# Splitting 4 KB of each row of one K load into sixteen small loads in a two-layer decode kernel

## The chip, the core and the metric

The kernel runs on one core of a Trainium2 chip. The core has a matrix engine (TensorE; PE in the profile, PEld for its weight loads), a vector engine (VectorE; DVE), a scalar engine (ScalarE; ACT), GpSimd (POOL) and SyncE (SP), which here does nothing but issue loads. Sixteen DMA engines move data between the chip's main memory (HBM) and the on-chip memory of 128 rows (partitions). The metric is the time of one execution in microseconds on the device; lower is better.

## What is computed

Two decode layers for 4 sequences, each an attention block with a cached K and V (8 groups of 4 query heads, 4096 cached positions, head size 128) and a gated feed-forward block, all in float32:

```python
def _A_ref(x, k_cache, v_cache, wq, wo):
    q = ...  # (x @ wq), split into 32 heads
    k = jnp.repeat(k_cache, rep, axis=1)
    v = jnp.repeat(v_cache, rep, axis=1)
    scores = jnp.einsum("bhqd,bhkd->bhqk", q, k) * (Dh ** -0.5)
    p = _softmax(scores, axis=-1)
    o = jnp.einsum("bhqk,bhkd->bhqd", p, v)
    return (lambda x, *d: x.transpose(*d))(o, 0, 2, 1, 3).reshape(B, Sq, Hq * Dh) @ wo
...
x = A_x
x = x + _A_ref(_layernorm(x, axis=-1), A_k_cache, A_v_cache, A_wq, A_wo)
x = x + _B_ref(_layernorm(x, axis=-1), B_w1, B_w3, B_w2)
x = x + _A_ref(_layernorm(x, axis=-1), A_k_cache, A_v_cache, A_wq, A_wo)
x = x + _B_ref(_layernorm(x, axis=-1), B_w1, B_w3, B_w2)
return x
```

Both layers use the same weights and the same cache. The cache is far larger than the on-chip memory: K and V are 8 MB each for one group, 128 MB in all, and are read once in each layer, apart from what is kept on chip between the layers.

## The kernel before

**The arena and the plan of loads.** All large data go through one tile, `arena`, of 212 KB in each of the 128 rows (lines 30, 31 and 46; `KB = 256` is a count of float32 elements, so 1 KB). The first 64 KB hold wq, the rest is handed out and taken back by `take` and `give`. A list, `plan` (lines 69 to 117), names every load in the order in which it is to be issued: source, the blocks (keys) that it brings, and a fixed place or none. `pump` (line 122) goes along this list: while there is room for the next load it issues it on SP (line 129) and notes where each key lies. When the last reader of a load has been issued, `done` or `vacate` gives the room back and calls `pump` again. The instructions are written out in this order by hand, and each engine runs its own in that order: SP issues one load after the other, and one that has to wait holds all that follow.

**The start of the plan.** Ahead of it ACT issues x without its first eight rows (line 156). Then SP issues the first 8 KB per row of wq, the first eight rows of x (line 132), the two halves of K of group 0 (32 KB per row each), the rest of wq (56 KB), K of group 1 (64 KB, 8 MB in all: the second K load, key `("k", 0, 1, 0)` and seven more), V of group 0, K of group 2 and so on. These up to K of group 1 find room at once; V of group 0 needs the room of K of group 0.

**Semaphores.** A load signals its landing on a semaphore. The framework gives the loads eight such semaphores in turn, in the order of the program, those of SP and the one of ACT together; the kernel does not say which load gets which, and the waits that come from it are the framework's.

**The work around it.** `project_q` (line 297) makes the first group's queries from the first part of wq; `scores` (line 330, matmuls in line 339) takes K of group 0, and then `q_product` (line 279, matmuls in line 283) makes the queries of the other seven groups when the rest of wq is there. Softmax (line 345) and the transposes of `turn_p` follow, then `scores` of group 1. From there on each group's scores are followed by `weigh` (line 374, matmuls in line 380) of the group before, with its V. A group's eight blocks of K are 8 KB per row each; in a block, the four sequences take 2 KB per row each.

Of the kernel before, what the change touches and what calls it, by code (L numbers as in the profile page):

```python
# [29 lines left out]
KB = 256  # L30
# [2 lines left out]
AGAIN = (0,)  # L33
SPLIT = 3
SCRATCH = 64


@with_exitstack
def tile_decode_layers(ctx: ExitStack, tc: tile.TileContext, x, kt, v, wq, wo, w1, w3, w2, out):
    nc = tc.nc  # L40
# [5 lines left out]
    arena = const.tile([P, ARENA * KB], F32, name="arena")  # L46
# [5 lines left out]
    def take(n, at=None):  # L52
        if at is not None and at < WO:
            return at
        for i, (lo, size) in enumerate(free):
            a = lo if at is None else at
            if lo <= a and a + n <= lo + size:
                free[i:i + 1] = [(p, s) for p, s in ((lo, a - lo), (a + n, lo + size - a - n)) if s]
                return a
        return None  # L60
# [61 lines left out]
    def pump():  # L122
        while state["next"] < len(plan):
            src, per, keys, at = plan[state["next"]]
            n = src.shape[-1] // KB
            a = take(n, at)
            if a is None:
                return
            nc.sync.dma_start(arena[:, a * KB:(a + n) * KB], src)
            i = state["next"]  # L130
            if i == 0:
                nc.sync.dma_start(xt[:8], x[:8])
            left[i] = (len(keys), a, n)
            for j, key in enumerate(keys):
                where[key] = (a + j * per, per, i)
            state["next"] += 1
# [5 lines left out]
    def done(*key):  # L142
        i = where[key][2]
        k, a, n = left[i]
        left[i] = (k - 1, a, n)
        if k == 1:
            give(a, n)
            pump()

    def vacate(*key):  # L150
        a, n, _ = where[key]
        give(a, n)
        pump()

    xt = const.tile([P, KC, B], F32, name="xt")
    nc.scalar.dma_start(xt[8:], x[8:])
    pump()

    ident = const.tile([P, P], F32, name="ident")
# [407 lines left out]
```

## Time and profile before

| | us |
|---|---|
| median of 3 runs | 711.67 |
| lowest and highest | 710.67, 712.11 |
| the profiled execution | 712.24 |
| its span, first to last instruction | 710.5 |
| PE busy in it | 417.6 (59%) |
| DVE busy | 76.3 (11%) |
| ACT busy | 38.6 (5%) |
| read from HBM | 299.90 MB, 422 GB/s over the span |

The profile is that of one execution. Its views are: a page with busy times, 40 equal slices of the span (busy shares in tenths, DMA share and GB/s), DMA queues and the chain of work that ended last, followed back from the last instruction; a view of instructions in order of time (start, duration, engine and line, operation, output and input, count); issues of loads with their size and the time from issue to landing, for any stretch; busy times by stretches; and who waited for whom. A "q" behind an engine's name is its sequencer, which issues loads and waits. All times are in microseconds from the first instruction.

### The profile page before, as it was taken

Reading aid. Unit: us, or ns where it says so; the run is one execution under the profiler, and the core shown is the slowest. Engines: PE = TensorE matmul, PEld = TensorE weight load, DVE = VectorE, ACT = ScalarE, POOL = GpSimd, SP = SyncE. Lnnn points to the kernel's source line nnn. Section 1 sums busy time; section 2 is a strip of 40 time slices with the busy share of each in tenths; the row PEclk is TensorE's granted clock in tenths of the full one; section 3 lists DMA queues with packets and bytes.
Section 4 is the critical chain, followed back from the end, with each engine's and each line's share of the span. In section 5 each row is a group of like instructions: output and inputs, shape, how many; then the busy total and the mean of one; then the engine's idle time right before and its main releaser. Section 6 shows DMA issues by size and latency. Waiting matters only on the chain.

```text
span 710.5 us, 7260 instructions
## 1 busy us (share of the span) xinstructions
PE 417.6 (59%) x3282; PEld 150.3 (21%) x3282; DVE 76.3 (11%) x270; ACT 38.6 (5%) x87; POOL 2.9 (0%) x10
## 2 busy tenths in 40 slices
PE   4545454546565554548578884265655636356878
PEld 2111121212121121212243221021211202121246
DVE  2010111111111010111011110111010011111111
ACT  0000000000000000001010000000000000001001
POOL 0000000000000000000000000000000000000000
PEclk9876776777676687779899997587787879788679
DMA  9999999999999999999999999999999999999995
GB/s 384 458 399 469 414 443 433 428 440 428 433 443 422 435 440 421 440 415 423 411 401 394 413 434 448 432 429 433 443 429 432 440 424 433 446 403 428 427 424 225
DMA packets 13862, 300.43 MB, mean 423 GB/s; under 512 B 1672, under 2 KB 1800, under 8 KB 6024
## 3 DMA queue, kind: packets, MB, share of 16 engines
q1 hardware_dynamic: 13696, 299.96, 98.7%
q8 instruction: 26, 0.43, 0.2%
q14 instruction: 5, 0.03, 0.0%
q10 hardware_dynamic: 135, 0.01, 0.0%
HBM read 299.90 MB, written 0.07 MB: 422 GB/s over the span
## 4 chain that ended last, share of the span: by engine, by line
DMA 69%; PE 26%; another core or an unknown queue 2%; DVE 1%; ACT 1%; issue 1%; SPq 0%; ACTq 0%; DVEq 0%
DMA arena<-in_v 29%; DMA arena<-in_kt 27%; PE o_ps L380 11%; PE s_ps L339 8%; DMA arena<-in_wq 6%; DMA arena<-in_wo 4%; DMA arena<-in_w 3%; PE q_ps L283 1%; PE d_ps L227 1%; PE s_ps L423 1%; ACT t L387 1%; PE m_ps L265 1%; PE x_ps L401 1%; PE o_ps L423 0%
## 5 line engine op out<-in xcount | busy, mean ns | idle before, releaser
L380 PE MATMUL o_ps<-arena,pT 128*32 128x512 f32 x1024 | 150.3, 737 | 144.6 <-DMA arena<-in_v 132.0
L339 PE MATMUL s_ps<-arena,qpad 128*32 128x512 f32 x1024 | 153.5, 755 | 89.9 <-DMA arena<-in_kt 89.9
L380 PEld LDWEIGHTS o_ps<-arena,pT 128*32 128x32 f32 x1024 | 38.2, 132 | 254.5 <-issue 224.8
L339 PEld LDWEIGHTS s_ps<-arena,qpad 128*32 128x32 f32 x1024 | 40.0, 134 | 186.6 <-issue 172.8
L389 DVE SCALAR_TENSOR_TENSOR t<-o_ps,parts,t 128x512 f32<-128x512 f32 x16 | 12.0, 751 | 266.7 <-PE o_ps L380 266.7
L346 DVE TENSOR_REDUCE top<-s_ps 128x1 f32<-128x512 f32 x16 | 11.1, 691 | 205.1 <-PE s_ps L339 205.1
L348 ACT ACTIVATE p<-s_ps,top 128x512 f32<-128x512 f32 x16 | 11.0, 687 | 315.1 <-DVE top L346 315.1
L392 PE MATMUL m_ps<-sel,t 128*128 128x16 f32 x128 | 17.0, 265 | 14.3 <-DVE t L389 14.2
L401 PE MATMUL x_ps<-arena,oT 128*4 128x256 f32 x256 | 18.8, 431 | 8.7 <-DMA arena<-in_wo 6.8
L387 ACT ACTIVATE t<-o_ps,parts 128x512 f32<-128x512 f32 x16 | 11.0, 687 | 212.6 <-PE o_ps L380 212.6
L283 PE MATMUL q_ps<-arena,xpad 128*32 128x512 f32 x112 | 14.8, 650 | 11.9 <-DMA arena<-in_wq 11.9
L392 PEld LDWEIGHTS m_ps<-sel,t 128*128 128x128 f32 x128 | 15.5, 191 | 29.1 <-DVE t L389 29.1
L227 PE MATMUL d_ps<-ident,rows 128*32 128x128 f32 x102 | 16.8, 288 | 0.0
L368 PE MATMUL t_ps<-ident,p 128*128 128x128 f32 x64 | 10.8, 293 | 4.5 <-ACT p L348 4.5
L227 PEld LDWEIGHTS d_ps<-ident,rows 128*32 128x32 f32 x102 | 11.7, 116 | 4.6 <-issue 0.5
L369 DVE COPY pT<-t_ps 128x512 f32<-128x512 f32 x16 | 11.0, 690 | 12.5 <-PE t_ps L368 12.5
L423 PE MATMUL s_ps<-arena,xpad 128*32 128x192 f32 (+1 forms) x128 | 9.7, 422 | 1.8 <-DMA arena<-in_w 1.5
L401 PEld LDWEIGHTS x_ps<-arena,oT 128*4 128x4 f32 x256 | 6.1, 92 | 17.3 <-DMA arena<-in_wo 7.3
L368 PEld LDWEIGHTS t_ps<-ident,p 128*128 128x128 f32 x64 | 7.6, 155 | 9.0 <-issue 5.1
L423 PE MATMUL o_ps<-arena,xpad 128*32 128x192 f32 (+1 forms) x128 | 8.1, 360 | 2.1 <-DMA arena<-in_w 2.0
L283 PEld LDWEIGHTS q_ps<-arena,xpad 128*32 128x32 f32 x112 | 3.5, 119 | 20.8 <-DMA arena<-in_wq 12.9
L401 PE MATMUL x_ps<-arena,hT 128*4 128x256 f32 x56 | 4.3, 379 | 2.8 <-DMA arena<-in_w 2.4
(96 smaller groups left out, 129.5 us busy)
## 6 DMA issues: line engine op xcount, KB each, us to landing
arena<-in_kt SPq DMA_DIRECT2D x4, 4096.0 KB, 21.0
arena<-in_v SPq DMA_DIRECT2D x4, 4096.0 KB, 40.2
arena<-in_kt SPq DMA_DIRECT2D x9, 1024.0 KB, 11.0
arena<-in_w SPq DMA_DIRECT2D x15, 512.0 KB, 7.4
arena<-in_wq SPq DMA_DIRECT2D x1, 7168.0 KB, 39.5
arena<-in_v SPq DMA_DIRECT2D x3, 2048.0 KB, 39.9
arena<-in_wo SPq DMA_DIRECT2D x1, 4096.0 KB, 25.2
arena<-in_kt SPq DMA_DIRECT2D x2, 2048.0 KB, 22.4
```

The lines of the kernel that those rows point to most:

```text
L227: nc.tensor.matmul(d_ps[0:32, :], rows, ident, start=True, stop=True)
L283: nc.tensor.matmul(ps[32 * k:32 * k + 32, :], xpad[:, k, lo:lo + 32], w[:, k, :], start=first, stop=last)
L339: nc.tensor.matmul(s_ps[32 * b:32 * b + 32, :], qpad[:, b, lo:lo + 32], k[:, j, :], start=(blk == 0), stop=(blk == NB - 1))
L346: nc.vector.tensor_reduce(top[:, 0:1], s_ps, axis=AX.X, op=ALU.max, negate=True)
L348: nc.scalar.activation(p, s_ps, AF.Exp, bias=top[:, 0:1], accum_out=l)
L368: nc.tensor.transpose(t_ps[:, i, :], p[:, i * P:(i + 1) * P], ident)
L380: nc.tensor.matmul(o_ps[32 * b:32 * b + 32, :], pT[:, i, 32 * b:32 * b + 32], w[:, b, :], start=(i == 0), stop=(i == NI - 1))
L387: nc.scalar.activation(t, o_ps, AF.Copy, scale=st["parts"][:, 0:1])
L389: nc.vector.scalar_tensor_tensor(t, o_ps, st["parts"][:, 1:2], t, op0=ALU.mult, op1=ALU.add)
L392: nc.tensor.matmul(flat(m), t[:, j * P:(j + 1) * P], sel[:, j].rearrange("p h b -> p (h b)"), start=(j == 0), stop=(j == 3))
L401: nc.tensor.matmul(x_ps[r:r + B, e * 256:e * 256 + 256], left(2 * i + n), w(n)[:, e * 256:e * 256 + 256], start=first, stop=last)
L423: nc.tensor.matmul(ps[32 * j:32 * j + 32, lo:lo + n], x32[:, k, :], w[:, j * n:(j + 1) * n], start=(k == 0), stop=(k == KC - 1))
```

## The change

One load of the plan, the second K load of layer 0, is issued in seventeen parts. The first 4 KB of each of its 128 rows go in sixteen loads, over rows 0 to 14, 15 to 28, and so on with 15, 14, 13 down to 1 row, and a last one of 8 rows (15 + 14 + ... + 1 + 8 = 128). The other 60 KB of each row follow in one load of 128 rows. Place in the arena, bytes and all other loads are as before. PE's waits follow from what its matmuls read.

```diff
+SHARED = ("k", 0, 1, 0)
...
             a = take(n, at)
             if a is None:
                 return
-            nc.sync.dma_start(arena[:, a * KB:(a + n) * KB], src)
             i = state["next"]
+            if keys[0] == SHARED:
+
+                r = 0
+                for m in (*range(15, 0, -1), 8):
+                    nc.sync.dma_start(arena[r:r + m, a * KB:(a + 4) * KB], src[r:r + m, 0:4 * KB])
+                    r += m
+                nc.sync.dma_start(arena[:, (a + 4) * KB:(a + n) * KB], src[:, 4 * KB:])
+            else:
+                nc.sync.dma_start(arena[:, a * KB:(a + n) * KB], src)
             if i == 0:
                 nc.sync.dma_start(xt[:8], x[:8])
```

## The prediction

> **What bounds the kernel now.** The page first: the rows by slices and the summary of the chain that ended last.
>
> ```profile
> span 710.5 us, 7260 instructions
> ...
> DMA  9999999999999999999999999999999999999995
> GB/s 384 458 399 469 414 443 433 428 440 428 433 443 422 435 440 421 440 415 423 411 401 394 413 434 448 432 429 433 443 429 432 440 424 433 446 403 428 427 424 225
> ...
> DMA 69%; PE 26%; another core or an unknown queue 2%; DVE 1%; ACT 1%; issue 1%; SPq 0%; ACTq 0%; DVEq 0%
> ```
>
> The DMA engines are busy in every slice but the last, and the chain is a row of loads. Next the table by stretches of time, for one long stretch of layer 0 and for the last microseconds of the loads.
>
> ```profile
> 82.00:324.00 242.00, 132.42 (x916) 41.74 (x916) 22.81 (x72) 12.19 (x27) 0.00 (x0) 0.74 1.00 432
> ...
> 700.00:704.20 4.20, 4.20 (x67) 3.56 (x55) 0.50 (x2) 0.29 (x2) 0.00 (x0) 1.00 0.54 213
> ```
>
> The last two columns are the busy share of the 16 DMA engines and GB/s. In 242 us the share is 1.00 at 432 GB/s, 27.0 GB/s for one engine: the queue never runs dry. The second row shows that the 16 engines do not finish together: 46% of 4.2 us, 1.9 us for the mean engine, is idle at the end because some are done before others. So two things can move the time: a gap in the stream of loads, which costs what it is long, and a better share-out among the engines, which can give 1.9 us at most.
>
> Then the place of the change: SP's issues, in the view in order of time, and the chain at that place.
>
> ```profile
> 0.74 0.37 SPq L129 DMA_DIRECT2D arena<-in_wq  x1
> 1.16 0.36 SPq L132 DMA_DIRECT2D xt<-in_x  x1
> 1.57 0.82 SPq L129 DMA_DIRECT2D arena<-in_kt  x2
> 2.43 0.45 SPq L129 DMA_DIRECT2D arena<-in_wq  x1
> 2.92 0.49 SPq L129 DMA_DIRECT2D arena<-in_kt  x1
> 30.06 0.33 SPq L129 DMA_DIRECT2D arena<-in_v  x1
> ```
> ```profile
> 2.43 39.46 DMA arena<-in_wq
> 41.90 0.04 issue
> 41.94 7.69 PE q_ps L283 x56
> ...
> 54.26 8.39 another core or an unknown queue
> 62.66 0.14 issue
> 62.79 10.01 PE s_ps L339 x64
> ```
>
> The second K load (8 MB, issued at 2.92) stands in the queue behind the rest of wq, which lands at 2.43 + 39.46 = 41.89. Its own bytes flow from then on and land at about 62.6, where PE starts its scores. Between 2.92 and 30.06 SP has nothing to issue.
>
> **What a load waits for before it is issued.** Eight completion semaphores are taken in turn by all loads, so the load eight places on takes the same one. Whether it waits for that, the middle of the kernel shows, where many loads are in flight. First the issue view of the stretch from 303 to 330.4 us (count, KB, us to landing; 1+1+2+1+1+2 = 8 loads), then single issues.
>
> ```profile
> arena<-in_wo SPq DMA_DIRECT2D x1, 4096.0 KB, 25.2
> arena<-in_v SPq DMA_DIRECT2D x1, 2048.0 KB, 27.0
> arena<-in_v SPq DMA_DIRECT2D x2, 1024.0 KB, 29.4
> arena<-in_wo SPq DMA_DIRECT2D x1, 2048.0 KB, 27.4
> arena<-in_wo SPq DMA_DIRECT2D x1, 1024.0 KB
> arena<-in_wo SPq DMA_DIRECT2D x2, 512.0 KB, 29.9
> ```
> ```profile
> 303.40 0.33 SPq L129 DMA_DIRECT2D arena<-in_v  x1
> ...
> 319.90 0.33 SPq L129 DMA_DIRECT2D arena<-in_wo  x1
> ...
> 330.42 0.33 SPq L129 DMA_DIRECT2D arena<-in_w  x1
> ...
> 345.10 0.33 SPq L129 DMA_DIRECT2D arena<-in_w  x1
> ```
>
> The load issued at 303.40 (2048 KB) lands at 303.40 + 27.0 = 330.40, and the ninth load, counted from it, goes out at 330.42. The one of 319.90 lands at 319.90 + 25.2 = 345.1, and the load eight places on goes out at 345.10. So a load is held until the load eight places ahead has landed, and SP, which issues in order, holds everything behind it.
>
> **The change, part by part.** Count all loads from the start: 0 is x on ACT, 1 the first wq, 2 the eight rows of x, 3 and 4 the halves of K 0, 5 the rest of wq. Before, the second K load is number 6. Now 6 to 21 are the sixteen pieces and 22 is the remaining 60 KB of each row. Piece j is load 5+j and waits for load j-3. Loads 1 to 5 and the second K load in the issue view, stretch by stretch:
>
> ```profile
> arena<-in_wq SPq DMA_DIRECT2D x1, 1024.0 KB, 4.8
> ...
> xt<-in_x ACTq DMA_DIRECT2D x1, 7.5 KB, 4.7
> ...
> arena<-in_kt SPq DMA_DIRECT2D x2, 4096.0 KB, 18.3
> ...
> arena<-in_wq SPq DMA_DIRECT2D x1, 7168.0 KB, 39.5
> ...
> arena<-in_kt SPq DMA_DIRECT2D x1, 59.7
> ```
>
> Pieces 1 and 2 go out at once, 3 to 5 at about 5.5, 6 and 7 after the halves of K 0 (median 18.3 us to landing). Piece 8 waits for load 5, the rest of wq: it can go out at 41.94 at the earliest. At that moment only pieces 1 to 7 stand behind wq in the queue, and an engine needs 4096 B / 27.0 GB/s = 0.152 us for a row, so 1.1 us at most. Then the queue is empty, and SP has nine small loads to issue before the large one.
>
> *Issue.* The eight rows of x (1.16) are followed by the next load at 1.57: 0.41 us. Over all loads of K the view by lines gives the shortest, median and longest issue in ns, and ACT's 120 rows of x took 0.66:
>
> ```profile
> L129 SPq DMA_DIRECT2D arena<-in_kt x33: 327/328/652, 1.6 to 605.8; - x33
> ```
> ```profile
> 0.73 0.66 ACTq L156 DMA_DIRECT2D xt<-in_x  x1
> ```
>
> So 0.33 and 0.66 are the bounds for one piece; I take 0.40, by the eight-row load, the nearest in shape. Nine issues: 3.6 us (3.0 to 5.9). Piece 16 waits for piece 8, and the remainder for piece 9; both were issued over 3 us before, and a load into an idle queue lands in about 1.6 us (the store of the result):
>
> ```profile
> out<-p SPq DMA_DIRECT2D x1, 64.0 KB, 1.6
> ```
>
> So neither holds. The large remainder is issued at 41.94 + 3.6 = 45.5.
>
> *First bytes.* The rates in 40 slices of 0.15 us of the stretch 0 to 6, and in slices of 0.03 of the stretch 41 to 42.2 with its packets (a packet counts where it starts):
>
> ```profile
> GB/s 1 0 0 0 0 0 0 0 0 0 0 273 328 164 165 166 329 385 330 550 276 550 275 550 330 495 330 385 495 276 770 1533 1369 0 218 0 0 0 437 1092
> ```
> ```profile
> GB/s 2185 0 8739 0 2185 2185 0 2185 4369 2185 2185 6554 0 2185 0 0 0 0 0 0 0 0 0 0 0 0 0 0 0 0 0 0 0 0 0 0 0 0 0 0
> DMA packets 31, 1.05 MB, mean 874 GB/s; under 512 B 15, under 2 KB 15, under 8 KB 15
> ```
>
> From the first row: issued at 0.74, first bytes in the twelfth slice (1.65 to 1.8), 1.0 us later. From the second: the engines turn from wq to K between 41.0 and 41.4, 41.2 in the mean, half a microsecond before SP can know that wq has landed. So the remainder flows from 46.5 where K flowed from 41.2: 5.3 us later. Of the load, 512 KB have moved in between; they would have taken 512 KB / 432 GB/s = 1.2 us. A restarted queue is slow at first: the 1 MB load needed 4.8 us, and 1.0 to the first byte, 2.4 for its bytes and the 0.5 us to the signal leave 0.9, part of it the x rows beside it; I take 0.3 (0 to 0.9).
>
> *Sum:* 5.3 - 1.2 + 0.3 = **4.4 us** (3.1 with issues of 0.33, the latest turn at 41.4 and no slow start; 7.6 with 0.66, the turn at 41.0 and 0.9). Since the queue is full from here to the end, nothing gives it back, and every later load and the work behind it moves by the same amount. The count of loads grows by 16, twice eight, so later loads stay on the same semaphores and meet the same waits.
>
> *Costed at nothing.* V 0 leaves SP at about 46 and not at 30.06, behind the pieces; its bytes follow K's, which flow until 64 or later, so there is 18 us of cover, and beyond that it would cost one for one. PE's q products (41.94) need wq alone. PE's first score matmul of this K now waits for 17 loads, all earlier than the remainder it waits for anyway. SP's seven early issues lie in its idle time before 30.06.
>
> *The share-out.* Sixteen loads of falling size put unlike numbers of rows on the engines. The Trainium skill (DMA: Bandwidth & Descriptors, "Why a DMA increments its semaphore by 16 and not by 1") says that such a load takes the largest number of engines up to 16 that divides its rows, and the lowest-numbered ones; by that the first engine moves 16 of these rows and the last none, where it was 8 each. No row here shows an engine's number. From rows: 128 rows over 16 engines are 8 for each before, and an engine that takes none, or one of every piece, takes 8 less or 8 more, which is 8 x 0.152 = 1.2 us. But a gap of 5.3 us has room even for one row of every piece (16 x 0.152 = 2.4 us), so every engine starts the remainder at the same time, and a head start is gone. I cost it at nothing; were a head start kept, it would be 1.2 us either way, which lies within the range.
>
> **Rivals.**
> *A. No gap, only the share-out (not slower).* Decides if all 17 issues are through before 41, that is, if the wait for the eighth load ahead does not hold here. For it: SP has 27 idle us, and 17 x 0.41 = 7 us would fit. Against it: 330.42 and 345.10. Price: the last engine is relieved by 1.2 us if it is the late one: 711.67 - 1.2 = 710.5; if not, up to 1.2 us more.
> *B. The pieces go one after another (the change does not do what it says).* They write the same columns of one tile; were each held until the one before has landed, 15 x 1.6 = 24 us would come in front of the remainder: 41.9 + 24 + 1.0 - 41.2 - 1.2 = 24.5, so 736. Against it: the two loads of x write different rows of one tile, and the second went out at 1.16 while the first landed at 0.73 + 4.7 = 5.4. The Trainium skill (same page, "Rules for kernel authors") warns that transfers under 64 KB are mostly overhead; its fit of 2.0 us for each would give 17 x 2.0 = 34 us, about 746, if they did not overlap.
> *C. The gap is partly given back.* The engines also fetch instructions, 16 KB at a time, each fetch on one of them, which falls behind the others:
>
> ```profile
> q8 instruction: 26, 0.43, 0.2%
> ```
>
> A fetch that falls into the gap costs no load, and if its engine is one of those that end last, part of the 1.9 us of unevenness comes back: at best 4.4 - 1.9 = 2.5, so 714.2.
>
> **How the numbers follow.** The profiled execution took 712.24 us (span 710.5 and 1.74 around it), 0.57 over the median of 711.67; 712.24 + 4.4 = 716.6 for such a run, and 711.67 + 4.4 = 716.1 for a median. I predict 716.1. Chances: forecast 0.80, A 0.09, B 0.03, C 0.08. The range runs from C (714.2) to the sum with dear issues, 711.67 + 7.6 = 719.3, and leaves out A and B. About 0.2% (1.4 us) can be told from no change. Slower by more: the forecast, B and nearly all of C, 0.89. Within it: most of A (-1.2 to +1.2) and a little of C, 0.08. Faster by more: 0.03, that part of A in which the whole 1.2 us is gained and the scatter of the runs (710.67 to 712.11) adds to it.
>
> **What would show it.** SP's issues: seven pieces before 26 us, the eighth at 41.9, the remainder near 45.5, V 0 right after. DMA rates: a hole from about 42.5 to 46.5. PE's scores of the second K at about 67.2 in place of 62.79, and the loads after that 4.4 us late and no more, to the end. If the eighth piece leaves before 41, the reason is wrong and A holds; if the shift at 67 is there but gone at 700, the engines have been evened out after all.

## The result and the profile after

| | before | after |
|---|---|---|
| median, us | 711.30 (4 runs) | 716.42 (4 runs) |
| lowest and highest | 710.67, 712.11 | 715.23, 717.03 |
| the profiled execution | 712.24 | 716.92 |
| its span | 710.5 | 715.1 |

The ratio after to before is 1.0067 (95% interval 1.0046 to 1.0088): slower by 4.8 us (3.3 to 6.3). The forecast was 4.4 us and 716.1. (The ratios and intervals here are taken over the runs; they are not exactly the quotients of the two medians.)

SP's issues of the changed kernel in the view in order of time; the pieces are L135, the 60 KB L137, V 0 the L139 at 46.13. The second fence has single issues from the same view (pieces 7 and 8), the third the pieces by line (ns: shortest, median, longest).

```profile
2.43 0.58 SPq L139 DMA_DIRECT2D arena<-in_wq  x1
3.05 42.57 SPq L135 DMA_DIRECT2D arena<-in_kt  x16
45.66 0.35 SPq L137 DMA_DIRECT2D arena<-in_kt  x1
46.13 0.36 SPq L139 DMA_DIRECT2D arena<-in_v  x1
```
```profile
25.05 0.27 SPq L135 DMA_DIRECT2D arena<-in_kt  x1
...
42.72 0.27 SPq L135 DMA_DIRECT2D arena<-in_kt  x1
```
```profile
L135 SPq DMA_DIRECT2D arena<-in_kt x16: 250/287/497, 3.0 to 45.3; - x16
```

Piece 7 leaves at 25.05, piece 8 only at 42.72, and between this and the remainder at 45.66 stand nine issues. PE's q products, which wait for the same wq, start at 42.75: piece 8 was held for wq's landing.

The queue in that time: rates of the stretch 36 to 56 us in 40 slices of 0.5 us, first before, then after. A row of 56 KB and more counts where it starts, so full flow shows as a burst every 2 to 2.5 us.

```profile
GB/s 0 1491 344 0 0 688 1147 0 0 0 2097 0 0 0 0 2097 0 0 0 131 1868 0 131 0 655 1311 0 0 131 1049 918 0 0 131 1180 786 0 131 0 1442
```
```profile
GB/s 0 1147 688 0 0 459 1376 0 0 0 254 172 139 98 25 123 82 41 57 25 66 1843 123 0 0 0 0 1843 123 0 0 492 1475 0 0 0 1720 246 0 0
```

Before, K's first rows start in the slice at 41.0. After, that slice begins a trickle of 25 to 254 GB/s, and the first large rows start in the slice at 46.5. In the table by stretches the hole is plain (last two columns: DMA share and GB/s):

```profile
43.50:46.50 3.00, 3.00 (x20) 0.79 (x16) 0.00 (x0) 0.00 (x0) 0.00 (x0) 0.50 0.25 66
```

What the hole does to the work behind it: PE's scores of the second and third K, before (the second is at 62.79, shown above) and after.

```profile
101.53 9.42 PE L339 MATMUL s_ps<-arena,qpad 128*32 128x512 f32 x64 [6.87 <-DMA arena<-in_kt]
```
```profile
66.31 9.92 PE L348 MATMUL s_ps<-arena,qpad 128*32 128x512 f32 x60 [7.86 <-DMA arena<-in_kt]
...
106.66 8.53 PE L348 MATMUL s_ps<-arena,qpad 128*32 128x512 f32 x64 [8.51 <-DMA arena<-in_kt]
```

They are 3.5 and 5.1 us late, and the end of the span 4.6. Between them the stream is as it was, and the end is as uneven:

```profile
82.00:324.00 242.00, 123.76 (x876) 39.84 (x880) 22.80 (x72) 10.01 (x24) 0.00 (x0) 0.74 1.00 433
...
705.00:709.20 4.20, 4.20 (x67) 3.58 (x63) 0.57 (x3) 0.08 (x1) 0.00 (x0) 1.00 0.49 193
```

433 GB/s after the hole, 432 before. In the last 4.2 us of the loads the engines are 49% busy, where it was 54%: the unlike shares of the pieces did not even them out.

That the second K is only 3.5 us late has a reason of its own. One instruction fetch moved. In the changed kernel the issue and queue view has it in the stretch 43.7 to 43.9, in the hole; before, it was in the stretch 46.2 to 46.4, in full flow.

```profile
q8 instruction: 1, 0.02, 29.2%
```

What that does shows where the engines turn from the second K to V 0: the rates in 40 slices of 0.06 us, before from 60.5 and after from 65.2.

```profile
GB/s 0 3277 4369 2185 1092 1092 2185 2185 0 0 0 0 0 0 0 0 0 0 0 0 0 0 0 0 0 0 0 0 1092 0 0 0 0 0 0 0 0 0 0 0
```
```profile
GB/s 0 0 0 0 0 0 2185 2185 3277 2185 4369 2185 1092 0 0 0 0 0 0 0 0 0 0 0 0 0 0 0 0 0 0 0 0 0 0 0 0 0 0 0
```

One row of 64 KB in one slice is 1092 GB/s. Before, fifteen engines turn between 60.56 and 60.98 and one only at 62.2, some 1.25 us later; after, all sixteen turn between 65.56 and 65.98. So the queue itself is 5.0 us late. PE waits for the last engine, which before was late on its own account, and so its scores are only 3.5 us late. The next fetch (in the stretch 87 to 88 before, 90 to 91 after) falls before K 2 has landed in both kernels, and there the scores are 5.1 us late.

### The profile page after: what moved, and what is told of

Read it like the earlier page. It is cut to its first block, busy times and chain, and to the rows that moved or that the text cites. A ratio compares the mean times of both kernels' runs of the same rounds, so it can differ in the third digit from the quotient of the medians.

```text
span 715.1 us, 7282 instructions
## 1 busy us (share of the span) xinstructions
PE 409.1 (57%) x3282; PEld 148.2 (21%) x3282; DVE 76.4 (11%) x270; ACT 38.6 (5%) x87; POOL 2.9 (0%) x10
## 4 chain that ended last, share of the span: by engine, by line
DMA 75%; PE 22%; ACT 1%; SPq 1%; issue 1%; DVE 0%; DVEq 0%; ACTq 0%
DMA arena<-in_v 35%; DMA arena<-in_kt 32%; PE o_ps L389 11%; PE s_ps L348 7%; DMA arena<-in_wo 4%; DMA arena<-in_w 3%; PE s_ps L432 1%; PE d_ps L236 1%; ACT t L396 1%; PE m_ps L274 1%; PE x_ps L410 0%; PE o_ps L432 0%; PE x_ps L489 0%; PE q_ps L292 0%; SPq L135 0%
## 5 line engine op out<-in xcount | busy, mean ns | idle before, releaser
L389 PE MATMUL o_ps<-arena,pT 128*32 128x512 f32 x1024 | 144.0, 710 | 151.5 <-DMA arena<-in_v 140.4
L348 PE MATMUL s_ps<-arena,qpad 128*32 128x512 f32 x1024 | 151.6, 741 | 94.4 <-DMA arena<-in_kt 94.4
L355 DVE TENSOR_REDUCE top<-s_ps 128x1 f32<-128x512 f32 x16 | 11.1, 691 | 207.6 <-PE s_ps L348 207.6
L378 DVE COPY pT<-t_ps 128x512 f32<-128x512 f32 x16 | 11.1, 691 | 12.6 <-PE t_ps L377 12.6
```

Source lines behind the costliest of these rows:

```text
L348: nc.tensor.matmul(s_ps[32 * b:32 * b + 32, :], qpad[:, b, lo:lo + 32], k[:, j, :], start=(blk == 0), stop=(blk == NB - 1))
L355: nc.vector.tensor_reduce(top[:, 0:1], s_ps, axis=AX.X, op=ALU.max, negate=True)
L378: nc.vector.tensor_copy(pT.rearrange("p i r -> p (i r)"), t_ps.rearrange("p i r -> p (i r)"))
L389: nc.tensor.matmul(o_ps[32 * b:32 * b + 32, :], pT[:, i, 32 * b:32 * b + 32], w[:, b, :], start=(i == 0), stop=(i == NI - 1))
```

## The experiments

The theory: SP may not issue a load before the load eight places ahead has landed; the eighth piece therefore waits for the rest of wq, and while SP then works through nine small issues the queue is empty. The rival: the pieces themselves, by their small rows or the unlike shares of the engines, cost the time. Each edit stands against the changed kernel, in the branch for the second K load; what each computes is the same. Each ratio is against the kernel before, run on the same chip.

**1. Sixteen even pieces.**

```diff
-                for m in (*range(15, 0, -1), 8):
-                    nc.sync.dma_start(arena[r:r + m, a * KB:(a + 4) * KB], src[r:r + m, 0:4 * KB])
+                for c in (0, 2):
+                    for r in range(0, P, 16):
+                        nc.sync.dma_start(arena[r:r + 16, (a + c) * KB:(a + c + 2) * KB], src[r:r + 16, c * KB:(c + 2) * KB])
```

> Sixteen pieces of 16 rows and 2 KB instead of the falling sizes: the same 512 KB, the same count of loads, but 8 KB more or less on no engine. Theory (SP holds the eighth piece until the rest of wq has landed, then nine issues empty the queue): the same gap, remainder issued near 45.7 us, first bytes near 46.6, time 715.5 to 717.0, that is 4 to 5.5 us over the kernel before. Rival (the unlike shares of the engines cost the time): back to the kernel before, 711 to 712.

Measured 718.89 against 711.58, ratio 1.0097 (1.0075 to 1.0119). The pieces by line and the issue of the remainder:

```profile
L135 SPq DMA_DIRECT2D arena<-in_kt x16: 310/418/1524, 2.9 to 47.0; - x16
```
```profile
47.50 0.42 SPq L136 DMA_DIRECT2D arena<-in_kt  x1
```

Without any unlike share the loss is no smaller, so the shares are not its cause. It is larger than the 715.5 to 717.0 expected: an issue of 16 rows takes 0.42 us where one of the falling sizes took 0.29, and one took 1.52. That is where the remainder's 47.50 in place of the 45.7 expected comes from.

**2. 24 pieces.**

```diff
-                for m in (*range(15, 0, -1), 8):
+                for m in (15, 7, 7, *range(13, 0, -1), *(1,) * 8):
```

> 24 pieces over the same 128 rows and 512 KB (15, 7, 7, 13 down to 1, and eight of one row). Theory: eight more issues of 0.33 us each stand between the landing of wq and the remainder, so the remainder is issued at 48.3 instead of 45.66 and the time is 2.6 us over the changed kernel, near 719.0 (718 to 720). Rival (rows of 4 KB or the shares cost it): bytes and rows are the same, so 716 to 717.

Measured 719.28 against 711.58, ratio 1.011 (1.009 to 1.0131): 7.8 us (6.4 to 9.3), 3.0 us more than the change cost. The remainder and PE's scores:

```profile
47.84 0.35 SPq L137 DMA_DIRECT2D arena<-in_kt  x1
```
```profile
68.52 6.68 PE L348 MATMUL s_ps<-arena,qpad 128*32 128x512 f32 x48 [10.58 <-DMA arena<-in_kt]
```

With the same bytes, eight more issues delay the remainder by 2.18 us and the scores by 2.21. The loss follows the number of issues.

**3 and 4. Six pieces, seven pieces.** With six the remainder is load 12, eight behind the second half of K 0; with seven it is load 13, eight behind the rest of wq.

```diff
-                for m in (*range(15, 0, -1), 8):
+                for m in (32, 32, 16, 16, 16, 16):
```
```diff
-                for m in (*range(15, 0, -1), 8):
+                for m in (32, 16, 16, 16, 16, 16, 16):
```

> Six pieces (32, 32 and four times 16 rows, 4 KB each) and the remainder: the remainder is load 12, and the load eight ahead of it is the second half of K 0, which lands at 25. Theory: all seven parts are issued before 26 us, the queue does not run empty, V 0 goes out at 30 as before, and the time is that of the kernel before: 711.3, within 0.7. Rival (splitting the load, or its small rows, cost the time): 1 to 4 us over the kernel before.

> Seven pieces (32 and six times 16 rows): one more than in the run with six, so the remainder is load 13, and the load eight ahead of it is the rest of wq. Theory: the remainder cannot be issued before wq lands at 42.3 to 42.7, first bytes at 43.4, which is 2.2 after the queue is done with wq, of which the pieces fill 1.2: 0.8 to 1.8 us over the kernel before, 712.1 to 713.1. Rival: as with six pieces, no step between the two.

Measured: six 712.99 (ratio 1.0016, 1.0000 to 1.0032), seven 712.85 (1.0019, 1.0003 to 1.0035), against 711.58. The remainder with six and with seven:

```profile
25.14 0.35 SPq L137 DMA_DIRECT2D arena<-in_kt  x1
```
```profile
42.56 0.35 SPq L137 DMA_DIRECT2D arena<-in_kt  x1
```

The wait is where the theory puts it: one piece more moves the remainder's issue by 17 us. With six, V 0 is load 13, and it is V 0 that waits for the rest of wq: it went out at 42.47 and not at 30 as expected. Its bytes follow K's, so it had time. But the times do not show the step. Six pieces in front of an early remainder cost about 1.1 us (0.0 to 2.3), which the theory had at nothing; seven cost 1.4 (0.2 to 2.5), within the stated range, but PE's scores start at 63.86 with six and at 64.03 with seven, so the seventh piece adds next to nothing. So small pieces have a price of their own when no hole covers them. The next runs look for it.

**5. One piece of 128 rows.**

```diff
-                for m in (*range(15, 0, -1), 8):
+                for m in (128,):
```

> The first 4 KB of the rows in one load of 128 rows, then the 60 KB: one extra load. Six loads of 16 and 32 rows without a gap cost 1.2 us on the first engine (remainder landing from 62.16 where the whole load landed from 60.90). If that is a price of each small load, about 0.2 us, this kernel is 0 to 0.3 us over the kernel before: 711.3 to 711.9. If it is a price of 4 KB rows, all of it stays: 712.5 to 713. Theory of the gap: no hole, V 0 is issued near 30 us.

Measured 711.70 against 711.30, ratio 1.0008 (0.9990 to 1.0026). PE's scores start at 62.85, where it was 62.79; with the six pieces it was 63.86:

```profile
62.85 9.70 PE L348 MATMUL s_ps<-arena,qpad 128*32 128x512 f32 x60 [4.93 <-DMA arena<-in_kt]
```

Rows of 4 KB cost nothing that can be seen when 128 of them are one load.

**6. The 60 KB first, the sixteen pieces behind.**

```diff
+                nc.sync.dma_start(arena[:, (a + 4) * KB:(a + n) * KB], src[:, 4 * KB:])
                 r = 0
                 for m in (*range(15, 0, -1), 8):
                     nc.sync.dma_start(arena[r:r + m, a * KB:(a + 4) * KB], src[r:r + m, 0:4 * KB])
                     r += m
-                nc.sync.dma_start(arena[:, (a + 4) * KB:(a + n) * KB], src[:, 4 * KB:])
```

> The same seventeen loads in the other order: the 60 KB first, the sixteen pieces behind. Theory: K's 60 KB follow wq without a gap, and the hole moves to where they end: the eighth piece waits for the 60 KB to land at about 61, nine issues of 0.33 us follow, V 0 is issued at about 64 and flows from 65 where it flowed from 60.5: 3.5 to 5 us over the kernel before, 715 to 716.5. Rival (a queue that is restarted with small rows before K 1 is what costs, at 42 us): the pieces are out of K's way, 711 to 713.

Measured 717.26 against 711.30, ratio 1.0082 (1.0064 to 1.0100). SP's issues of the pieces and of V 0:

```profile
3.60 61.45 SPq L136 DMA_DIRECT2D arena<-in_kt  x16
65.17 0.35 SPq L139 DMA_DIRECT2D arena<-in_v  x1
```

The hole has moved from the front of K 1 to the front of V 0, and the loss is there again. It is not bound to the place at 42 us. V 0 is issued 1.2 us later than expected (piece 8, which waits for the 60 KB, left at 62.21 and not at 61), and 717.3 lies above the expected 715 to 716.5.

**7 and 8. Unlike shares without a gap.**

```diff
-                for m in (*range(15, 0, -1), 8):
+                for m in (120, 8):
```
```diff
-                for m in (*range(15, 0, -1), 8):
-                    nc.sync.dma_start(arena[r:r + m, a * KB:(a + 4) * KB], src[r:r + m, 0:4 * KB])
+                for m in (15, 14, 13, 11, 11, 64):
+                    nc.sync.dma_start(arena[r:r + m, a * KB:(a + 8) * KB], src[r:r + m, 0:8 * KB])
                     r += m
-                nc.sync.dma_start(arena[:, (a + 4) * KB:(a + n) * KB], src[:, 4 * KB:])
+                nc.sync.dma_start(arena[:, (a + 8) * KB:(a + n) * KB], src[:, 8 * KB:])
```

> The first 4 KB as 120 rows and 8 rows, then the 60 KB: unlike shares without a gap. By the split into 15 and 8 engines, one engine takes eight rows less (1.2 us) and eight take one more (0.15 us). If the engine that is relieved is the one that ends last, the time falls by up to 1.2 us against the run with one piece; if not, it stays or rises by up to 0.2. Gap theory: no hole, 711.0 to 712.

> Six pieces of 15, 14, 13, 11, 11 and 64 rows, 8 KB each, and 56 KB: unlike shares (nine rows on the engines that take most, four on the one that takes least, so 5 x 0.30 = 1.5 us between them, 1.2 less than an even share for the last) without a gap. Gap theory: V 0 does not wait for a string of issues; near the run with six even pieces, 712 to 713.5, if the shares do nothing; down to 711 if the engines that take less are the ones that end last.

Measured: two pieces 713.15 (ratio 1.0024, 1.0009 to 1.0039), six unlike pieces 715.26 (1.0049, 1.0034 to 1.0064), against 711.30. Neither gains; both lose, and both more than expected (711.0 to 712 and 712 to 713.5). The stretch 43 to 46 us of the second, and its last microseconds of loads:

```profile
43.00:46.00 3.00, 3.00 (x20) 0.63 (x16) 0.00 (x0) 0.00 (x0) 0.00 (x0) 0.51 1.19 213
...
704.70:708.90 4.20, 4.20 (x103) 3.75 (x98) 0.18 (x1) 0.00 (x0) 0.00 (x0) 1.00 0.58 223
```

There is no hole: the engines are busy (a share over 1 means that the rows of an engine overlap), but they move 213 GB/s, half the rate. And 58% busy at the end against 54% before is hardly more even. Sharing out rows in this way costs more than it could give. The two pieces are slow as well: in 40 slices of 0.15 us from 41 to 47, their rates are 137 to 273 GB/s between 41.45 and 42.65.

```profile
GB/s 164 765 382 246 164 137 218 191 218 191 273 328 601 191 1720 1720 437 1638 410 0 0 0 0 0 0 0 0 0 410 0 0 0 0 410 1229 2458 1638 410 0 0
```

**9. Pieces on two queues.** Eight of fourteen falling pieces go on GpSimd, so that no wait for wq stands in front of the remainder.

```diff
-                for m in (*range(15, 0, -1), 8):
-                    nc.sync.dma_start(arena[r:r + m, a * KB:(a + 4) * KB], src[r:r + m, 0:4 * KB])
+                for j, m in enumerate((15, 14, 13, 12, 11, 10, 9, 8, 7, 6, 5, 4, 3, 11)):
+                    queue = nc.sync if j < 6 else nc.gpsimd
+                    queue.dma_start(arena[r:r + m, a * KB:(a + 4) * KB], src[r:r + m, 0:4 * KB])
```

> Fourteen pieces of falling size over the same 4 KB of each row (15, 14, 13, 12, 11, 10 on SP; 9, 8, 7, 6, 5, 4, 3 and 11 rows on GpSimd, whose loads have eight semaphores of their own), then the 60 KB on SP. The pieces and the unlike shares stay, the wait for the rest of wq in front of the remainder goes: the remainder is load 12 on SP's count and is issued before 27 us. Theory: no hole between 43 and 46; what is left is what small pieces cost without a gap (1.3 us with six even ones, up to 3.3 with six unlike ones of 8 KB): 712.5 to 715, and the first score matmul of this K before 66. Rival (the pieces and shares themselves cost it all): 716 to 717 as with the change.

Measured 736.08 against 711.50, ratio 1.0344 (1.0321 to 1.0366). The expected 712.5 to 715 is missed by far, and the run answers another question than it was made for. GpSimd's issues, the last of the eight, and what stood behind it on GpSimd:

```profile
1.25 0.69 POOL L136 DMA_DIRECT2D arena<-in_kt  x1 [0.80 <-POOLq L568]
8.81 0.52 POOL L136 DMA_DIRECT2D arena<-in_kt  x1 [6.88 <-issue]
...
62.55 0.52 POOL L136 DMA_DIRECT2D arena<-in_kt  x1 [8.61 <-issue]
63.06 0.22 POOL masks.py:197 MEMSET ident<- 128x128 f32 x1
```

From one of its issues to the next 7.6 to 11.1 us went by, though the instruction itself is shown with 0.5, and the identity matrix, on which all first work hangs, was behind them on the same engine. Whether the full queue beside them is the reason, no run shows. So the time says nothing of the wait. One half of the test did come out: on SP alone the remainder was load 12, and it went out early, as the count by eight says.

```profile
26.42 0.35 SPq L138 DMA_DIRECT2D arena<-in_kt  x1
```

**10 and 11. Four pieces of neighbouring rows, four of every fourth row.**

```diff
-                for m in (*range(15, 0, -1), 8):
-                    nc.sync.dma_start(arena[r:r + m, a * KB:(a + 4) * KB], src[r:r + m, 0:4 * KB])
+                for r in range(0, P, 32):
+                    nc.sync.dma_start(arena[r:r + 32, a * KB:(a + 4) * KB], src[r:r + 32, 0:4 * KB])
```
```diff
-                for m in (*range(15, 0, -1), 8):
-                    nc.sync.dma_start(arena[r:r + m, a * KB:(a + 4) * KB], src[r:r + m, 0:4 * KB])
+                for r in range(4):
+                    nc.sync.dma_start(arena[r::4, a * KB:(a + 4) * KB], src[r::4, 0:4 * KB])
```

> Four pieces of 32 neighbouring rows, 4 KB each, and the 60 KB; no gap (remainder is load 10). Beside the run with the same pieces strided. If neighbouring rows share ways into the on-chip memory, the 512 KB flow at about half rate and the load lands 0.8 to 1.3 us later than the whole one: 711.8 to 713. If it is a price of each load (0.2 us), 0.8.

> Four pieces of every fourth row (32 rows each, spread over all 128), otherwise as the run with four blocks: same bytes, same count, same share of each engine. If neighbouring rows were the cost, most of it goes: 0 to 0.5 us over the kernel before, first score matmul at least 0.5 us earlier than with the four blocks. If it is a price of each load, as with the blocks.

Measured: blocks 713.05 (ratio 1.0027, 1.0014 to 1.0041), strided 711.99 (1.0012, 0.9993 to 1.0030), against 711.50. The intervals overlap, so by the times the two cannot be told apart; the traces can tell them apart at this place. (The profiled executions took 713.89 and 715.54 us; only their first part is compared.) Rates from 41 to 47 us in slices of 0.15 us, and PE's scores, blocks and then strided:

```profile
GB/s 109 246 355 383 328 109 273 164 246 191 328 246 628 2185 1284 901 819 847 0 410 0 0 0 0 0 0 0 0 0 0 0 1229 2458 1638 819 410 0 0 0 0
```
```profile
63.90 8.55 PE L346 MATMUL s_ps<-arena,qpad 128*32 128x512 f32 x56 [5.60 <-DMA arena<-in_kt]
```
```profile
GB/s 55 164 410 355 383 382 410 410 1174 737 3386 1666 27 27 27 27 410 0 0 0 0 0 0 410 410 3277 2048 0 0 0 0 410 0 0 0 0 0 0 0 819
```
```profile
62.74 9.36 PE L346 MATMUL s_ps<-arena,qpad 128*32 128x512 f32 x60 [4.96 <-DMA arena<-in_kt]
```

The strided pieces flow at 355 to 410 GB/s and the large rows begin in the slice at 42.2; the blocks flow at 109 to 383, and the large rows begin at 42.8 to 42.95. The scores start 1.16 us apart, and the strided kernel is where the kernel before was (62.79). So, in this pair of traces, it is not the small load that costs, but that its rows are neighbours. The Trainium skill (SBUF — State Buffer, "Door 1: The DMA port swizzle") has the rule: the rate of a load depends on how many of the on-chip memory's 16 ports its rows reach, and four neighbouring rows share one. By that page 32 neighbours reach eight ports and every fourth row reaches all; the two traces agree in direction, with 109 to 383 against 355 to 410 GB/s. It is not the whole account: run 7, with 120 neighbouring rows in one piece, was slow too (137 to 273), and no run shows why.

**12. Seven strided pieces.**

```diff
-                for m in (*range(15, 0, -1), 8):
-                    nc.sync.dma_start(arena[r:r + m, a * KB:(a + 4) * KB], src[r:r + m, 0:4 * KB])
+                for r, step in ((0, 4), (1, 8), (5, 8), (2, 8), (6, 8), (3, 8), (7, 8)):
+                    nc.sync.dma_start(arena[r::step, a * KB:(a + 4) * KB], src[r::step, 0:4 * KB])
```

> Seven pieces as in the run with seven (one of 32 rows, six of 16), but of every fourth or eighth row, so that they flow at full rate as the four strided ones did (load landing from 61.03). With neighbouring rows the seventh piece cost only 0.6 us over six, because slow pieces filled the hole. Theory: the remainder again waits for the rest of wq, is issued at 42.3 to 42.7 and flows from 43.3; full-rate pieces are done at 42.4, so a hole of about 0.9 to 1.2 us shows: PE's first score matmul of this K at 63.2 to 64.2 against 62.74 with four strided pieces, time 0.5 to 1.7 us over the kernel before. Rival (no wait, only the rate of the pieces): as with four strided pieces, 62.6 to 62.9.

Measured 712.95 against 712.39, ratio 1.0000 (0.9984 to 1.0017). The remainder's issue and PE's scores:

```profile
42.22 0.33 SPq L135 DMA_DIRECT2D arena<-in_kt  x1
```
```profile
63.42 9.01 PE L346 MATMUL s_ps<-arena,qpad 128*32 128x512 f32 x56 [7.66 <-DMA arena<-in_kt]
```

In the trace the step is there, 63.42 against 62.74, in the stated range; in the time it is not seen, though 0.5 to 1.7 us were expected (0.0, with an interval from -1.1 to 1.2). A hole of about 1 us lies below what these runs can tell. No version tried beats the kernel before.

## Why the prediction was right

The step that carried it was the wait for the load eight places ahead, read in the trace of before from two pairs of times. It held: pieces 1 to 7 out by 25.05, piece 8 with the landing of wq, V 0 right behind the remainder. What the runs showed of the terms:

| term | forecast | measured |
|---|---|---|
| piece 8 is issued | 41.94 | 42.72 |
| nine issues | 9 x 0.40 = 3.6 | 42.72 to 45.66 = 2.94 |
| remainder is issued | 45.5 | 45.66 |
| first large rows | 46.5 | 46.5 to 47.0 (one slice) |
| slow start of the remainder | 0.3 (0 to 0.9) | about 0.7 |
| queue behind the remainder | 5.3 - 1.2 + 0.3 = 4.4 late | 5.0 late |
| whole effect | +4.4 | +4.8 (3.3 to 6.3), span +4.6 |

The slow start is read from the rates in slices of 0.5 us: the first burst of the remainder stands at 46.5, the second at 49.5, 3.0 us later, and the next follow after about 2.3. The 5.0 is the turn to V 0 (65.56 where it was 60.56). With the restart at its measured size the sum would have been 5.3 - 1.2 + 0.7 = 4.8; the interval of the times holds 4.4 and 5.0 alike.

Two terms were off by 0.7 to 0.8 us and cancel, which is luck. The issues were dearer in the forecast, taken from an eight-row load at the start; pieces of falling size take 0.25 to 0.50, 0.29 in the median. And wq landed later than before: PE's q products, which need it, start at 42.75 and not at 41.94. In the runs with several pieces right behind wq the remainder, where it waited for wq, went out at 42.2 to 42.6; with the 60 KB behind wq the q products started at 41.98, and nothing was late there. That the pieces queued behind it delay the signal fits all these, but no run changed that alone.

One sum was wrong: the lower end of the 4.4 is, from its own terms, 41.94 + 3.0 + 1.0 - 41.4 - 1.2 = 3.3 and not 3.1. The stated range did not use it.

*What was costed at nothing.* V 0's later issue, PE's wait for 17 loads and the early issues cost nothing that the trace shows: after the hole the stream runs at 433 GB/s. The share-out is as forecast without effect, and for the reason given: the hole lets all engines start together, and the end is no more even (0.49). What the forecast did not have is the low rate of such pieces: it let pieces 1 to 7 flow for 1.1 us at most after 41.2, and they trickle until about 43.5. With the change it is hidden, since the pieces are through before the remainder can start; without the hole PE's scores start 1.1 us later (runs 3 and 10; the times say 1.1 and 1.9), and run 8 lost 3.5 us.

*Rival A* (no gap) falls with the issue at 42.72 and with runs 2 and 6, where the loss follows the issues and moves with the hole. It would not have given its 1.2 us either: in runs 7 and 8 unlike shares without a gap lost 1.7 and 3.5 us. *Rival B* (one piece after another) falls with issues 0.3 us apart, at either of its prices. *Rival C* (part is given back) came true for a while: the fetch in the hole made the second K only 3.5 us late, and by the third K it was gone. The forecast of 67.2 for the scores of the second K (66.31) missed this; "4.4 us late and no more" holds from the third K on, within 0.7.

Left open: which engines end last, so it is not known whether a share-out at full rate could even them out; why wq's landing is late with pieces behind it; and why two pieces of 120 and 8 rows cost 1.7 us.

## What to carry to other kernels

Where loads take their completion semaphores in turn, count what is in flight: a string of small loads behind a long one is held until the long one has landed, and then the queue runs dry for as long as the string takes to issue. Count, for the large load behind a split, how many places it stands behind the long load ahead. While these are fewer than eight it is not held, and what is left is the price of the pieces themselves: 0.6 to 1.9 us in runs 3, 5, 7, 10 and 11 (in 5 and 11 not to be told from nothing), 3.5 in run 8. From eight on it is held and the queue can run dry; where it does, each piece still to be issued costs one issue: 0.27 us with pieces of one row (run 2), 0.33 with the change, 0.57 in run 1. And if a load must be split by rows, spreading the rows of each piece over the whole width kept the rate up in the one pair of traces that tried it.

## What the runs showed of the hardware

Pieces of neighbouring rows flow slower: 213 GB/s with busy engines in run 8 and 109 to 383 in run 10, where four strided pieces of 32 rows kept 355 to 410 (run 11) and the full stream has 432. An issue on SP took 0.42 us for 16 rows of 2 KB (run 1) and 0.25 to 0.29 for the pieces of 1 to 8 rows behind wq (the change). Eight loads issued on GpSimd beside a full queue went out 7.6 to 11.1 us apart (run 9). After an instruction fetch in full flow one engine of sixteen was 1.25 us behind the others, and the landing with it (the kernel before, at 62.2); a fetch in the hole left none behind.
